# Making all queries early, so that their tiles become slots for VectorE's exponentials, and splitting the end of a kernel of attention and a state-space layer over two engines and two queues

## The chip, the cores and the metric

The kernel runs on one core of one Trainium2 chip. The metric is the device time of one execution in microseconds (us), as the median of several executions. Beside the time there is a trace of one execution of each kernel. Its span, from the first to the last instruction, is shorter than the device time of the same execution (before: 754.8 us).

PE is the tensor engine, PEld its weight loads, DVE is VectorE, ACT is ScalarE, POOL is GpSimd, SP is the engine that issues most DMAs (607 of 611 before).

## The reference, cut to what matters

Two independent layers of 2048 positions and width 640 are computed and laid side by side: a state-space layer (A) and attention (B) with 32 heads of 20 that share one key and one value. (The code is shortened here, not word for word.)

```python
def _B_ref(x, wq, wk, wv, wo):
    q = (x @ wq).reshape(B, S, H, Dh).transpose(0, 2, 1, 3)
    k, v = x @ wk, x @ wv
    p = _softmax(jnp.einsum("bhqd,bkd->bhqk", q, k) * (Dh ** -0.5), axis=-1)
    o = jnp.einsum("bhqk,bkd->bhqd", p, v)
    return o.transpose(0, 2, 1, 3).reshape(B, S, H * Dh) @ wo

return jnp.concatenate([_A_ref(...), _B_ref(...)], axis=-1)     # _A_ref: a linear recurrence over the 2048 positions
```

The scores are 32 x 2048 x 2048 values. In the kernel they are 2048 tiles of 128 keys x 512 queries, and each tile needs an exponential.

## The kernel before: the parts that matter

The kernel is built by a small scheduler of its own. It simulates the five engines with a duration for each operation, writes down the order in which operations start, and emits that order with semaphores. It draws 24 random plans and keeps the one that it reckons shortest. So a change in one place can move instructions everywhere, and the order on each engine is fixed when the kernel is built.

```python
        best = None
        for seed in range(self.PLANS):
            plan = copy.copy(self)
            plan.s = Schedule(seed)
            plan.program()
            try:
                plan.s.run()
            except RuntimeError:
                continue
            end = max(op.end for op in plan.s.order)
            if best is None or end < best[0]:
                best = (end, plan)
        return best[1]
```

Exponentials are made in two ways. ScalarE takes two or three tiles in one instruction, straight from a group of three PSUM banks. VectorE takes single tiles: it writes `max(score + 16256, 0)` as a 16-bit integer, which is read as a bf16 number near the exponential, and three more copies of it, each shifted by a constant. The four versions are each multiplied with their own share of the values, so their errors cancel. Each version needs a holder (`DR`) until the tensor engine has read it.

```python
    CHUNKS = (3, 3)
    MISC = 1
    NPT = 24
    NOP = 7
    NRD = 3
    NDS = 18
    SHARE = 0.25

    SHIFTS = ((0, 0.2421875), (32, 0.201171875), (64, 0.169921875), (96, 0.142578125))
# ...
    def fill_d(self, op, m, bank=None):
        h = self.d_free()[0]
        self.d_count += 1
        b, kc, j = self.score(op, m, bank.ap, bank)
        n = len(self.SHIFTS)
        h.taken, h.left, h.users = True, n, []
        key = f"DR{h.index}"
        first = self.dve(self.ts(p.DR[:, h.index, :], bank.ap, 16256.0, 0.0, ALU.add, ALU.max), 663, deps=[op],
                         reads=[bank.key], writes=[key], prio=self.P1OWN if own else self.P1)
# ...
    def want_d(self, taken=0, own=0):
        s = self.s
        if self.tile_n >= NTILE - 8 or self.d_count + taken + own + 1 > self.SHARE * (self.tile_n - 16):
            return False
        if len(self.d_banks()) <= taken or self.behind():
            return False
        return len(self.d_free()) > taken + own + len(self.SHIFTS) - 1
```

`want_d` says when a tile may go to VectorE: not in the last 8 tiles, only up to a quarter of all tiles (`SHARE`), and only when a holder is free for the first version and each of its copies. There are 18 holders. The copies are made in pairs, by VectorE or by GpSimd.

Queries are made from `xbT` (the transposed input) and `wqf` in four blocks of 512 positions, each one some 300 to 450 tiles ahead of its use, through the buffer `QP`:

```python
        for qb in range(NQB):
            for blk in range(NC):
                t = -98 + blk if qb == 0 else (qb - 1) * 512 + 60 + 40 * blk
```

The last of them comes at tile 1244 of 2048. Until then the three buffers stay in use.

Groups of heads are normalised through DRAM, all but the last one. At the end, the last accumulator is copied out of PSUM into `pvsb`, its sums are turned and inverted on chip, and it is normalised in one piece. Five output tiles are evicted and sent from one queue:

```python
                return e.reciprocal(p.rdT[:], bank.cols(0, 16))
        r = self.dve(rc, 170, deps=[m1], reads=[bank.key], writes=[f"rdT{slot}"], prio=0.45)
        spread = bass.AP(tensor=p.rdT, offset=0, ap=[[16, 128], [1, 16], [0, 32]])
        self.spread_op[b] = self.dve(lambda e: e.tensor_copy(p.rdX[:], spread), 350, deps=[r],
                                      reads=[f"rdT{slot}"], writes=[f"rdX{slot}"], prio=1)
# ...
    def norm_task(self, b, bank):
        p = self
        slot = b % 2
        src = p.pvsb[:, slot, :]
        fns = [self.mm(bank.cols(128 * i, 128 * i + 128),
                       p.rdX[:, 4 * i:4 * i + 4, :].rearrange("p j d -> p (j d)"), p.ident[:], True, True)
               for i in range(4)]
        m2 = self.pe(fns, 4 * 65, deps=[self.spread_op[b], self.c_op["ident"]] + bank.last, prio=1.5,
                     reads=[f"rdX{slot}", "ident"], writes=[bank.key])
        d = self.dve(self.tt(src, src, bank.ap, ALU.mult), 610, deps=[m2],
                     reads=[bank.key, f"pvsb{slot}"], writes=[f"pvsb{slot}"], prio=self.EV)
# ... in finish(), for the last five output tiles:
        if end in (4, 1, 3):
            ev = self.act(lambda e: e.activation(st, bank.ap, ACT.Copy), 600, ...)
        else:
            ev = self.dve(lambda e: e.tensor_copy(st, bank.ap), 620, ...)
# ...
        self.stage_dma[key] = self.dma(fns, 131072, f"out{key}", deps=[ev], reads=[key], prio=1)
```

Of the kernel before, what the change touches and what calls it, by code (L numbers as in the profile page):

```python
# [412 lines left out]
class Build:  # L413
# [5 lines left out]
    NDS = 18  # L419
# [16 lines left out]
    def build(self):  # L436
        nc = self.nc
        with ExitStack() as o:
# [10 lines left out]
            with ExitStack() as p2:  # L449
# [11 lines left out]
                shares.update({f"CT{tb}_{c}": [f"xn{tb}"] for tb in range(2) for c in range(NC)})  # L461
                em = Emitter(nc, plan.s.order, [b.key for b in plan.banks], shares)
# [39 lines left out]
    def alloc(self, o):  # L502
        sb = self.sb
        self.xbT = sb(o, "xbT", [128, NC, S], BF16)
# [5 lines left out]
        self.wqf = sb(o, "wqf", [128, NC * 640], BF16)  # L510
# [6 lines left out]
        self.DR = sb(o, "DR", [128, self.NDS, 512], I16)  # L517
        self.VZ = sb(o, "VZ", [128, 32], BF16)
        self.WO = sb(o, "WO", [128, NC, 640], BF16)
        self.WOt = sb(o, "WOt", [128, 640], BF16)  # L520
# [5 lines left out]
        self.QP = sb(o, "QP", [128, NC, 512], BF16)  # L526
# [10 lines left out]
        self.rdT = sb(o, "rdT", [128, 16], BF16)  # L537
        self.rdX = sb(o, "rdX", [128, 16, 32], BF16)
# [97 lines left out]
    def program(self):  # L636
# [8 lines left out]
        self.evac_op, self.norm_op, self.spread_op = {}, {}, {}  # L645
# [24 lines left out]
        self.s.spawn(self.late_loads())  # L670
        self.free_banks.remove(self.pvbank)
# [4 lines left out]
        self.s.sources["dve"].append(self.copy_source)  # L676
        self.s.sources["pool"].append(self.pool_source)
# [34 lines left out]
    def constants(self):  # L712
# [14 lines left out]
        def select(t, pattern, op, v, base, mult, dur):  # L727
# [24 lines left out]
              for i in range(1, 12)]  # L752
# [11 lines left out]
        self.c_op["WOt"] = self.dve(lambda e: e.memset(p.WOt[:], 0.0), 250, writes=["WOt"], prio=2.5,  # L764
                                    gate=lambda: self.tile_n > 300)

    def loads(self):
# [30 lines left out]
        fns = [lambda e, j=j: e.dma_start(p.WOt[32 * j:32 * j + 20, :], self.wo[560 + 20 * j:580 + 20 * j, :]) for j in range(4)]  # L798
        self.wot_op = self.dma(fns, 102400, "wot", reads=["WOt"], writes=["WOt"], deps=[self.c_op["WOt"]])
# [426 lines left out]
    def want_own(self):  # L1226
        if self.tile_n >= NTILE - 8 or self.d_count + 1 > self.SHARE * (self.tile_n - 16) or self.behind():
            return False
        if sum(1 for o in self.firsts if o.start is None) >= self.WAITING:
            return False  # L1230
        self.firsts = [o for o in self.firsts if o.start is None]
        return len(self.d_free()) > len(self.SHIFTS) - 1
# [82 lines left out]
    def want_d(self, taken=0, own=0):  # L1315
        s = self.s
        if self.tile_n >= NTILE - 8 or self.d_count + taken + own + 1 > self.SHARE * (self.tile_n - 16):
            return False
        if len(self.d_banks()) <= taken or self.behind():
            return False  # L1320
        return len(self.d_free()) > taken + own + len(self.SHIFTS) - 1
# [32 lines left out]
    def fill_d(self, op, m, bank=None):  # L1354
# [12 lines left out]
        first = self.dve(self.ts(p.DR[:, h.index, :], bank.ap, 16256.0, 0.0, ALU.add, ALU.max), 663, deps=[op],  # L1367
# [11 lines left out]
    def pv_entry(self, b, kc, j, k, h, op):  # L1379
        self.pvq[b][j].append((self.VS[:, k, kc, 0:32], kc, self.DR[:, h.index, :].bitcast(BF16), f"DR{h.index}", op, h, "VS"))  # L1380
# [33 lines left out]
    BACKLOG = 9  # L1414

    def pool_source(self):
# [3 lines left out]
        if not can or len(self.d_free()) < 2:  # L1420
            return None
# [7 lines left out]

    def copy(self, op, k, tiles, pool=False):  # L1430
# [5 lines left out]
        def at(x):  # L1436
            if len(x) == 1:
                return p.DR[:, x[0], :]
            return bass.AP(tensor=p.DR, offset=512 * x[0], ap=[[512 * p.NDS, 128], [512 * (x[1] - x[0]), 2], [1, 512]])
        if pool:  # L1440
            def words(x):
                return bass.AP(tensor=p.DR, offset=512 * x[0], ap=[[512 * p.NDS, 128], [512 * (x[1] - x[0]), 2], [1, 512]]).bitcast(I32)
            add = bass.AP(tensor=p.step, offset=k, ap=[[4, 128], [0, 2], [0, 256]])
            op.fns.append(self.tt(words(dst), words(src), add, ALU.add))
            op.reads.append("step")
        else:
# [43 lines left out]
    def pv(self, op, b, group):  # L1490
# [14 lines left out]
        if self.pv_filled[b] == 64 and not any(self.pvq[b]) and not any(self.d_left[b, j] for j in range(4)):  # L1505
            self.pv_b += 1
            slot = b % 2
            ev = self.dve(lambda e: e.tensor_copy(p.pvsb[:, slot, :], bank.ap), 620, deps=[op], reads=[bank.key],
                          writes=[f"pvsb{slot}"], prio=self.PVEV,
                          gate=lambda: b < 2 or self.s.done(self.scat_op[b - 2]))  # L1510
            self.evac_op[b] = ev
            if b < NQB * NGG - 1:
                self.normalize(b, ev)
            self.pv_gate = [ev]
# [17 lines left out]
    def normalize(self, b, ev):  # L1532
# [6 lines left out]
        sd = o = self.dma(lambda e: e.dma_start(sums, p.pvsb[20:117:32, slot, :]), 4096, f"sum{slot}", land=self.LATE_DMA, deps=[ev], reads=[pv],  # L1539
# [11 lines left out]
        for blk, parts in self.rows_of(b).items():  # L1551
            at, rd = (NC * qb + blk) % self.NOP, (NC * qb + blk) % self.NRD
            zero = []
            if b == NQB * NGG - 2 and blk == NC - 1:
# [4 lines left out]
            self.scat_op[b].append(self.dma(fns, 1024 * sum(x[3] for x in parts), f"OP{at}", issue=770.0, deps=[ev] + zero, reads=[pv], writes=[f"OP{at}"],  # L1559
# [8 lines left out]
            if rows == 128 or zero:  # L1568
                self.norm_op[NC * qb + blk] = self.dve(
                    self.tt(p.OP[0:rows, at, :], p.OP[0:rows, at, :], p.rdP[0:rows, rd, :], ALU.mult), 350,  # L1570
                    deps=self.rd_op[NC * qb + blk], port=True, reads=[f"OP{at}", f"rdP{rd}"], writes=[f"OP{at}"], prio=self.EV)
# [7 lines left out]
    def den_task(self, b, bank):  # L1579

        p = self
        slot = b % 2
        src = p.pvsb[:, slot, :]
        m1 = self.pe([self.mm(bank.cols(4 * i, 4 * i + 4), src[:, 128 * i:128 * i + 128], p.E1[:], True, True)
                      for i in range(4)], 4 * 65, deps=[self.evac_op[b], self.c_op["E1"]] + bank.last, prio=1.5,
                     reads=[f"pvsb{slot}", "E1"], writes=[bank.key])

        def rc(e):
            with p.nc.allow_low_precision("bf16 reciprocal of softmax denominator"):
                return e.reciprocal(p.rdT[:], bank.cols(0, 16))  # L1590
        r = self.dve(rc, 170, deps=[m1], reads=[bank.key], writes=[f"rdT{slot}"], prio=0.45)
        spread = bass.AP(tensor=p.rdT, offset=0, ap=[[16, 128], [1, 16], [0, 32]])
        self.spread_op[b] = self.dve(lambda e: e.tensor_copy(p.rdX[:], spread), 350, deps=[r],
                                      reads=[f"rdT{slot}"], writes=[f"rdX{slot}"], prio=1)
        yield lambda: r.start is not None
        bank.last = [r]
        self.give(bank)

    def norm_task(self, b, bank):
        p = self  # L1600
        slot = b % 2
        src = p.pvsb[:, slot, :]
        fns = [self.mm(bank.cols(128 * i, 128 * i + 128),
                       p.rdX[:, 4 * i:4 * i + 4, :].rearrange("p j d -> p (j d)"), p.ident[:], True, True)
               for i in range(4)]
        m2 = self.pe(fns, 4 * 65, deps=[self.spread_op[b], self.c_op["ident"]] + bank.last, prio=1.5,
                     reads=[f"rdX{slot}", "ident"], writes=[bank.key])
        d = self.dve(self.tt(src, src, bank.ap, ALU.mult), 610, deps=[m2],
                     reads=[bank.key, f"pvsb{slot}"], writes=[f"pvsb{slot}"], prio=self.EV)
        self.norm_op[NC * NQB] = d  # L1610
# [4 lines left out]
    def o_task(self, qb, k, bank):  # L1615
# [6 lines left out]
        for blk in range(NC):  # L1622
            at = (NC * qb + blk) % self.NOP
            steps.append((NC * qb + blk, p.OP[:, at, :], p.WO[:, blk, :], [f"OP{at}", "WO"]))
        if last:
            slot = (NQB * NGG - 1) % 2
            steps.append((NC * NQB, p.pvsb[:, slot, :], p.WOt[:], [f"pvsb{slot}", "WOt"]))

        def part(i, prev):
# [3 lines left out]
            for ts in range(4) if k == 4 else [k]:  # L1633
                out, ww = (bank.cols(128 * ts, 128 * ts + 128), w[:, 512:640]) if k == 4 else (bank.ap, w[:, 0:512])
                fns.append(self.mm(out, src[:, 128 * ts:128 * ts + 128], ww, i == 0 and ts in (0, k), end))
            return self.pe(fns, 4 * 65 if k == 4 else self.mmt(512), deps=[self.norm_op[n], self.wo_op, self.wot_op] + bank.last,
                           prev=prev, prio=1.4 if last and end else 2.5 if last else self.task_prio(),
                           reads=keys, writes=[bank.key])
        for i in range(len(steps)):
            if last:  # L1640
                yield lambda: steps[i][0] in self.norm_op
            prev = part(i, prev)
# [6 lines left out]
        self.give(bank)  # L1649

    def finish(self, prev, rows, bank, ops, end=None):
# [10 lines left out]
        if end in (4, 1, 3):  # L1662
            ev = self.act(lambda e: e.activation(st, bank.ap, ACT.Copy), 600, deps=[prev], reads=[bank.key], writes=[key], prio=1)
        else:
# [8 lines left out]
        self.stage_dma[key] = self.dma(fns, 131072, f"out{key}", deps=[ev], reads=[key], prio=1)  # L1673
# [375 lines left out]
    SSM_FROM, SSM_TO, Y_STEP, GRACE = 260, 1850, 20, 40  # L2049
    unit_due = {}  # L2050

    def background(self):
        T = self.tasks
        T.append((-100, 1, lambda: all((0, c) in self.xb_op for c in range(NC)), lambda bank: self.qt_task(bank)))
        for qb in range(NQB):
            for blk in range(NC):
                t = -98 + blk if qb == 0 else (qb - 1) * 512 + 60 + 40 * blk
                T.append((t, 1, lambda qb=qb, blk=blk: self.q_ready(qb, blk), lambda bank, qb=qb, blk=blk: self.q_task(qb, blk, bank)))
            T.append((t + 0.5, 0, lambda qb=qb: self.row_ready(qb), lambda bank, qb=qb: self.row_task(qb, bank)))
        for b in range(NQB * NGG):  # L2060
            if b == NQB * NGG - 1:
                T.append((64 * (b + 1), 0, lambda b=b: self.den_ready(b), lambda bank, b=b: self.den_task(b, bank)))
                T.append((64 * (b + 1), 0, lambda b=b: b in self.spread_op and self.s.done([self.spread_op[b]]),
                          lambda bank, b=b: self.norm_task(b, bank)))
        for qb in range(NQB):
            for k in range(5):
                T.append((512 * (qb + 1) + 30 + 40 * k if qb < NQB - 1 else NTILE - 8, 2, lambda qb=qb: self.o_ready(qb),
                          lambda bank, qb=qb, k=k: self.o_task(qb, (4, 0, 1, 2, 3)[k], bank)))
        jobs = []
# [25 lines left out]
    def den_ready(self, b):  # L2095
        return b in self.evac_op and self.s.done([self.evac_op[b]])

    def o_ready(self, qb):
        blks = range(NC if qb < NQB - 1 else 1)
# [97 lines left out]
```

## Time and profile before

| | before |
|---|---|
| time, median of 4 | 758.48 us (758.28 to 758.72) |
| span of the traced execution | 754.8 us |
| first exp starts | 21.57 us |
| exps on ScalarE | 419 of two tiles, 247 of three: 1579 tiles |
| tiles on VectorE | 469 |
| last exp ends | 742.29 us |

Two lines of the page of the kernel before. The first has the busy time of each engine, its share of the span and its instructions. The second has the chain of work that ended last, by engine.

```profile
PE 711.4 (94%) x11441; PEld 260.3 (34%) x11442; DVE 649.7 (86%) x1301; ACT 732.2 (97%) x692; POOL 432.4 (57%) x455
...
ACT 80%; PE 16%; DVE 3%; issue 1%; POOL 0%; DVEq 0%
```

ScalarE is busy nearly all the time, and following the waits back from the last instruction one is on ScalarE for 80% of the span. So ScalarE's stream of exps sets the time, and what other engines do costs time only where it makes an exp start late.

The groups of instructions of the kernel before, by shape. The columns are line, engine, operation, tiles, shapes and count, then busy time and mean ns of one, then the idle time before them and what ended it.

```profile
L628 POOL TENSOR_TENSOR DR<-DR,step 128x512 int32<-128x512 int32 x407 | 413.2, 1042 | 292.8 <-DVE DR L633 197.5 <-PE MB L618 29.1 <-DVE g L1950 19.2
L1177 ACT ACTIVATE PR<-SC 128x1024 bf16<-128x1024 f32 x419 | 407.9, 1149 | 3.2 <-PE SC L618 2.8 <-PE MB L618 0.2
L1177 ACT ACTIVATE PR<-SC 128x1536 bf16<-128x1536 f32 x247 | 351.7, 1603 | 0.4 <-PE MB L618 0.4
L633 DVE TENSOR_SCALAR DR<-SC 128x512 int16<-128x512 f32 x404 | 272.5, 687 | 53.3 <-PE SC L618 40.1 <-PE MB L618 8.3 <-POOL DR L628 1.1
...
L633 DVE TENSOR_SCALAR DR<-DR 128x1024 int16<-128x1024 int16 x269 | 106.8, 442 | 11.4 <-PE MB L618 10.4
...
L633 DVE TENSOR_SCALAR DR<-MB 128x512 int16<-128x512 f32 x65 | 44.1, 679 | 2.4 <-PE MB L618 2.3
```

The mean of an exp (1149 ns) is not what it costs, because consecutive exps overlap: the shortest of two tiles lasts 1.017 us, longer than the 0.904 from its start to the next one's. The start times in the trace say more: back to back, an exp of two tiles is followed by the next after 0.904 us and one of three after 1.331 us. The 666 exps thus need 419 x 0.904 + 247 x 1.331 = 707.5 us. From the first exp's start to the last one's it took more than that: summed over all pairs of neighbours, the starts came 12.8 us later than back to back. I call these 12.8 us the late starts. The remaining 12.6 us are what comes after the last exp.

That end is in the timeline of the kernel before. The columns are start, duration, engine, line and operation with tiles, then in brackets the idle time before and its releaser. An `x12` stands for twelve instructions in a row.

```profile
740.20 4.00 DVE L633 TENSOR_SCALAR DR<-DR 128x1024 int16<-128x1024 int16 x12 [0.22 <-PE MB L618]
...
744.77 0.69 DVE L1508 CAST pvsb<-MB 128x512 bf16<-128x512 f32 x1 [0.58 <-PE MB L618]
...
746.28 0.43 DVE L1593 COPY rdX<-rdT 128x512 bf16<-128x512 bf16 x1
...
747.26 0.69 DVE L628 TENSOR_TENSOR pvsb<-pvsb,SC 128x512 bf16<-128x512 bf16 x1 [0.23 <-PE SC L614]
...
748.46 0.60 ACT L1663 ACTIVATE PR<-MB 128x512 bf16<-128x512 f32 x1 [6.17 <-PE MB L614]
...
748.68 1.34 DVE L1665 CAST PR<-SC 128x512 bf16<-128x512 f32 x2 [0.73 <-PE SC L614]
...
749.09 2.43 SPq L1672 DMA_DIRECT2D out_dram<-PR  x5
...
749.76 0.60 ACT L1663 ACTIVATE PR<-SC 128x512 bf16<-128x512 f32 x1 [0.21 <-PE SC L614]
```

The last exp ended at 742.29. VectorE still made copies until 744.2, so the accumulator could only be copied out at 744.77. The reciprocal, a spread copy and a multiplication follow in a chain, then five evictions until 750.36, while one queue issues the five outputs one after the other until 751.5.

### The profile page before, as it was taken

Reading aid. Unit: us, or ns where it says so; the run is one execution under the profiler, and the core shown is the slowest. Engines: PE = TensorE matmul, PEld = TensorE weight load, DVE = VectorE, ACT = ScalarE, POOL = GpSimd, SP = SyncE. Lnnn points to the kernel's source line nnn. Section 1 sums busy time; section 2 is a strip of 40 time slices with the busy share of each in tenths; the row PEclk is TensorE's granted clock in tenths of the full one; section 3 lists DMA queues with packets and bytes.
Section 4 is the critical chain, followed back from the end, with each engine's and each line's share of the span. In section 5 each row is a group of like instructions: output and inputs, shape, how many; then the busy total and the mean of one; then the engine's idle time right before and its main releaser. Section 6 shows DMA issues by size and latency. Waiting matters only on the chain.

```text
span 754.8 us, 26719 instructions
## 1 busy us (share of the span) xinstructions
PE 711.4 (94%) x11441; PEld 260.3 (34%) x11442; DVE 649.7 (86%) x1301; ACT 732.2 (97%) x692; POOL 432.4 (57%) x455
## 2 busy tenths in 40 slices
PE   9998988888999999999899999998999999999996
PEld 4332222244433532333343333332443233343323
DVE  7879999999988698788989889889898999887885
ACT  5899999999999999999999999999999999999994
POOL 3775565503755255587555675545665656756781
PEclk9999999999999999999999999999999999999999
DMA  9436544311220011101100101112000010000001
GB/s 199 87 89 151 118 120 87 72 21 25 46 47 15 23 32 56 41 18 29 41 16 12 39 30 38 36 31 50 15 19 14 12 39 17 23 19 26 14 25 42
DMA packets 78484, 34.59 MB, mean 46 GB/s; under 512 B 59080, under 2 KB 78368, under 8 KB 78368
## 3 DMA queue, kind: packets, MB, share of 16 engines
q1 hardware_dynamic: 77036, 32.76, 17.9%
q8 instruction: 91, 1.49, 0.8%
q10 hardware_dynamic: 1332, 0.13, 0.2%
q14 instruction: 25, 0.20, 0.1%
HBM read 11.59 MB, written 9.76 MB: 28 GB/s over the span
## 4 chain that ended last, share of the span: by engine, by line
ACT 80%; PE 16%; DVE 3%; issue 1%; POOL 0%; DVEq 0%
ACT PR L1177 79%; PE MB L618 5%; PE SC L618 5%; PE MB L614 4%; PE SC L614 1%; DVE DR L633 1%; DVE prod L628 1%; DVE CT L628 0%; DVE W L633 0%; PE SC L902 0%; DVE g L1950 0%; DVE CT L632 0%; POOL DR L628 0%; DVE CA L628 0%; DVE CA L632 0%
## 5 line engine op out<-in xcount | busy, mean ns | idle before, releaser
L1177 ACT ACTIVATE PR<-SC 128x1024 bf16<-128x1024 f32 (+1 forms) x666 | 718.0, 1317 | 3.6 <-PE SC L618 2.8
L628 POOL TENSOR_TENSOR DR<-DR,step 128x512 int32<-128x512 int32 x407 | 413.2, 1042 | 292.8 <-DVE DR L633 197.5
L633 DVE TENSOR_SCALAR DR<-SC 128x512 int16<-128x512 f32 x404 | 272.5, 687 | 53.3 <-PE SC L618 40.1
L618 PE MATMUL SC<-QT,KT 32*128 32x512 bf16 x1983 | 260.6, 384 | 31.9 <-ACT PR L1177 25.9
L618 PE MATMUL MB<-DR,VS 128*32 128x512 bf16 x1876 | 223.0, 384 | 0.9 <-POOL DR L628 0.5
L618 PE MATMUL MB<-PR,VP 128*32 128x512 bf16 x1579 | 208.8, 384 | 2.6 <-ACT PR L1177 1.1
L618 PEld LDWEIGHTS SC<-QT,KT 32*128 32x128 bf16 x1983 | 66.9, 91 | 257.7 <-ACT PR L1177 185.7
L633 DVE TENSOR_SCALAR DR<-DR 128x1024 int16<-128x1024 int16 (+1 forms) x324 | 120.7, 421 | 13.3 <-PE MB L618 12.1
L618 PEld LDWEIGHTS MB<-DR,VS 128*32 128x32 bf16 x1876 | 55.8, 94 | 67.1 <-issue 38.2
L618 PEld LDWEIGHTS MB<-PR,VP 128*32 128x32 bf16 x1579 | 53.7, 94 | 56.8 <-issue 36.2
L614 PE MATMUL MB<-CT,W 128*32 128x320 bf16 (+2 forms) x1040 | 52.2, 301 | 0.7 <-DVE prod L628 0.4
L633 DVE TENSOR_SCALAR DR<-MB 128x512 int16<-128x512 f32 x65 | 44.1, 679 | 2.4 <-PE MB L618 2.3
L614 PE MATMUL MB<-xaT,BT 128*32 128x256 bf16 x800 | 33.3, 274 | 0.0
L618 PE MATMUL MB<-KT,VZ 128*32 128x256 bf16 x628 | 33.0, 274 | 0.0
L614 PE MATMUL MB<-xaT,BA 128*32 128x256 bf16 x800 | 32.3, 274 | 0.3 <-DVE DR L633 0.3
L628 DVE TENSOR_TENSOR prod<-MB,tab 128x1024 bf16<-128x1024 f32 x20 | 24.4, 1220 | 8.7 <-PE MB L614 8.7
L614 PE MATMUL MB<-CA,W 128*32 128x512 bf16 (+1 forms) x640 | 30.7, 302 | 0.6 <-DVE prod L628 0.5
L614 PEld LDWEIGHTS MB<-CT,W 128*32 128x32 bf16 x1040 | 21.2, 96 | 18.9 <-issue 10.0
L1665 DVE CAST stg<-MB 128x512 bf16<-128x512 f32 x35 | 23.9, 682 | 3.0 <-PE MB L614 2.6
L1950 DVE TENSOR_TENSOR_SCAN g<-sc,hst,prod 128x256 bf16<-128x256 f32 x30 | 26.3, 883 | 0.0
L618 PE MATMUL MB<-QT,KT 32*128 32x512 bf16 x65 | 24.9, 384 | 0.0
L614 PE MATMUL MB<-WO,OP 128*32 128x128 bf16 (+1 forms) x560 | 24.5, 290 | 0.0
(150 smaller groups left out, 443.1 us busy)
## 6 DMA issues: line engine op xcount, KB each, us to landing
out_dram<-stg SPq DMA_DIRECT2D x31, 128.0 KB, 1.8
qd<-QP SPq DMA_DIRECT2D x20, 128.0 KB, 1.9
QT<-qd SPq DMA_DIRECT2D x28, 80.0 KB
OP<-pvsb SPq DMA_DIRECT2D x108, 20.0 KB
rdP<-recs SPq DMA_DIRECT2D x108, 20.0 KB
W<-in_A_B_re_dram SPq DMA_DIRECT2D x10, 160.0 KB, 2.7
W<-in_A_B_im_dram SPq DMA_DIRECT2D x10, 160.0 KB, 3.2
lbd<-W SPq DMA_DIRECT2D x10, 160.0 KB, 2.0
```

The lines of the kernel that those rows point to most:

```text
L614: r = e.matmul(out[32 * j:32 * j + 32], lhsT=lhsT[:, 32 * j:32 * j + 32], rhs=rhs, start=start, stop=stop, tile_position=(0, 32 * j), skip ...
L618: return lambda e: e.matmul(out, lhsT=lhsT, rhs=rhs, start=start, stop=stop, **kw)
L628: return lambda e: e.tensor_tensor(out, a, b, op)
L633: return lambda e: e.tensor_scalar(out, a, s1, s2, op0=op0, op1=op1)
L1177: ex = self.act(lambda e: e.activation(dst, t[:, 0:512 * n], ACT.Exp, scale=1.0 / UNIT), 0.8333 * 512 * n + 64, table="exp", deps=[op], re ...
L1665: ev = self.dve(lambda e: e.tensor_copy(st, bank.ap), 620, deps=[prev], reads=[bank.key], writes=[key], prio=self.EV, gate=(lambda: last.e ...
L1950: o = self.dve(lambda e, ri=ri, init=init: e.tensor_tensor_scan(p.g[:, u, ri, :], rdec, p.prod[:, 1, 0, ri, :], init, ALU.mult, ALU.add), ...
```

## The change

Its intent: all four blocks of queries are due by tile 250. Then `wqf`, `QP` and most of `xbT` are dead, and 21 more holders are laid over them (`MORE`), beside two more of the old kind. With 41 holders instead of 18, VectorE can take more tiles. At the end, the last two head groups are normalised on chip, three of the five last outputs are computed early but for the last group and kept as partial sums, the last copy out of PSUM and the last normalisation are halved, VectorE takes no tile in the last 20, and two of the five outputs go out from ScalarE's queue.

```diff
-    NDS = 18
+    NDS = 20
+    MORE = 21
@@ alloc: one buffer for xbT, wqf, QP and the holders; the added holders lie over the first three
+        self.BIG = sb(o, "BIG", [128, ends[3]], BF16)
+        self.xbT = self.BIG[:, 0:ends[0]].rearrange("p (c n) -> p c n", c=NC)
+        self.wqf = self.BIG[:, ends[0]:ends[1]]
+        self.QP = self.BIG[:, ends[1]:ends[2]].rearrange("p (c n) -> p c n", c=NC)
+        self.dr_at = [ends[2] + 512 * i for i in range(self.NDS)]
+        # ... 10 in xbT, 6 in wqf, 5 in QP
@@ new: the holders join once the last queries are made
+    def more(self):
+        yield lambda: NQB - 1 in self.row_mm and self.s.done([self.row_mm[NQB - 1]]) \
+            and all(self.s.done([self.qd_op[NQB - 1, i]]) for i in range(NC))
+        self.dhold += [Holder(self.NDS + i) for i in range(self.MORE)]
@@ want_own, want_d
-        if self.tile_n >= NTILE - 8 or ...
+        if self.tile_n >= NTILE - self.LAST or ...          # LAST = 20
@@ background
-                t = -98 + blk if qb == 0 else (qb - 1) * 512 + 60 + 40 * blk
+                t = -98 + blk if qb == 0 else self.Q_FROM[qb] + self.Q_STEP * blk   # (0, 30, 110, 190), 15
-    SSM_FROM, SSM_TO, Y_STEP, GRACE = 260, 1850, 20, 40
+    SSM_FROM, SSM_TO, Y_STEP, GRACE = 260, 1780, 20, 40
@@ pv: the last accumulator leaves PSUM in two halves
+                self.evac_op[b] = [
+                    self.act(lambda e: e.activation(p.pvsb[:, slot, 0:256], bank.cols(0, 256), ACT.Copy), 390, ...),
+                    self.dve(lambda e: e.tensor_copy(p.pvsb[:, slot, 256:512], bank.cols(256, 512)), 350, ...)]
-            if b < NQB * NGG - 1:
+            if b < NQB * NGG - 2:
                 self.normalize(b, ev)
@@ den_task: no spread copy; the matrix unit reads the reciprocals with a step of 0; two halves
-        self.spread_op[b] = self.dve(lambda e: e.tensor_copy(p.rdX[:], spread), 350, ...)
+                    col = bass.AP(tensor=p.rdT, offset=16 * slot + 4 * i + j, ap=[[32, 128], [0, 32]])
@@ finish
-        if end in (4, 1, 3):
+        if end in (1, 3):
             ev = self.act(lambda e: e.activation(st, bank.ap, ACT.Copy), 600, ...)
+        elif end is not None:
+            ev = self.dve(self.tt(st, bank.ap, self.partial(end), ALU.add), 630, ...)
-        ... self.dma(fns, 131072, f"out{key}", deps=[ev], reads=[key], prio=1)
+        ... self.dma(fns, 131072, f"out{key}", deps=[ev], reads=[key], prio=1, eng=ev.eng if end == 1 or end == 3 else "sp")
```

Cut: the shifting of two head groups into the small weight tile `WOt`, the bookkeeping of two keys for a halved tile, `o_task` with its early part, a stop of GpSimd's copies in the last 10 tiles (`POOL_LAST`), a copy on ScalarE after the last tile.

## The prediction

> **What bounds it now.** The span is 754.8 us. On the page ACT is 97% busy (PE 94%, DVE 86%, POOL 57%), and the chain that ended last is 79% the exp line. From the trace: first exp at 21.57 us, last exp ends at 742.29. Of 2048 score tiles ScalarE takes 1579, as 419 exps of two tiles and 247 of three. Back to back they start 0.904 and 1.331 us apart: 707.6 us; the other 12.8 us are late starts (3.6 us of them idle in the waits). [...] Only moving tiles off ScalarE, or shortening the 12.5 us after the last exp, helps. The other 469 tiles are VectorE's: one 0.687 us op from PSUM and three shifted copies, made in pairs by DVE (0.42 us) or POOL (1.04 us).
>
> **What the change does** (instruction order of both builds): early queries free the input, wq and query buffers, so holders go from 18 to 41. VectorE tiles rise from 469 to 498 (cap 512). ScalarE has 470 exps of two, 203 of three, one of one: 424.9 + 270.2 + 0.5 = 695.6 us, 12.0 less, all on the chain. DVE gains 29 x 0.687 = 20 us of first ops, 40 pair copies (17 us), three partial-output evictions: about +40, to 690 of 743 us, 93%. POOL goes from 407 to 418 pairs. More pairs are not adjacent, which costs nothing: both forms took 0.42 us.
>
> **The end** (timeline): from last exp to the cast of pvsb 2.5 us, as 12 copies still run; cast 0.69, sums, reciprocal, 0.43 spread copy, 0.69 multiply; output matmuls and five evictions to 750.36; five output DMAs issued in a row on one queue, the last 0.74 us after the last eviction; then 3.3 us to landing and end. After: VectorE tiles stop 20 before the end instead of 8 (-1.0), the cast is halved over two engines (-0.3), no spread copy (-0.5), three evictions become adds to early partial sums but stay a chain of three on DVE (0), three queues (-0.5). About 2.3 us less.
>
> **Against it.** DVE at 93% has half its former slack. PE scores of a slot wait for the DVE op that empties its third bank (34 us of such waits, hidden behind the other slot). Queries are packed early, near where PE was 99% busy (200 to 300 us, table of windows). I allow 3 us of new late exps. [...]
>
> **Sum.** 21.57 + 695.6 + 12.8 + 3 + 10.2 = 743.2 us of span; the timed median lies 3.8 us above the profiled span, so 747.0 us. Range 743.0 to 752.0. Chances: over 2% faster 0.16, within 2% 0.83, slower 0.01.
>
> **What would show each step.** Exp counts 470/203; last exp ending near 733 us; late starts 13 to 19 us; DVE near 690 us busy; 10 to 11 us after the last exp; output issues on ACT's queue too.
>
> **What would make it wrong.** DVE late in bursts, with runs of two-tile exps each needing 0.69 us plus copies within 0.904 us: then PE waits, exps start late, and the 12 us shrink. If fewer matmuls compete late, the lags may fall and the gain pass 2%. The three DVE adds may stretch the end.

The sum is: 743.2 us of span, 747.0 us of time. The 3 us of late exps in it is an allowance of mine, and the 0.5 us for the exp of one tile an estimate (0.904 less the 0.427 from two tiles to three); no trace showed them.

## The result, and the profile after

The change takes 748.25 us in the median of four (747.54 to 750.88) against 758.48 for the kernel before. The ratio is 0.9871, with a 95% interval of 0.9847 to 0.9896. Here and below a ratio is the mean time of one kernel's runs over that of the other's of the same rounds, so it is not quite the ratio of the medians quoted. It is 1.3% faster, within the 2% that count as the same, and within the predicted range.

The page of the kernel after, the same two lines:

```profile
PE 710.7 (95%) x11325; PEld 256.3 (34%) x11325; DVE 665.3 (89%) x1360; ACT 721.6 (97%) x700; POOL 446.0 (60%) x466
...
ACT 70%; PE 26%; DVE 3%; issue 0%; DVEq 0%
```

ScalarE still sets the time, though the chain now passes the tensor engine more often (26% instead of 16%). VectorE is 15.6 us busier than before, not 40.

The groups of instructions of the kernel after. `BIG` is now the buffer of the holders.

```profile
L1197 ACT ACTIVATE PR<-SC 128x1024 bf16<-128x1024 f32 x470 | 445.0, 1107 | 6.6 <-PE SC L635 6.1 <-PE MB L635 0.2
L645 POOL TENSOR_TENSOR BIG<-BIG,step 128x512 int32<-128x512 int32 x418 | 426.7, 1050 | 270.1 <-DVE BIG L650 116.6 <-DVE g L2025 73.3 <-PE MB L635 19.2
L650 DVE TENSOR_SCALAR BIG<-SC 128x512 int16<-128x512 f32 x456 | 303.7, 686 | 41.7 <-PE SC L635 34.9 <-PE MB L635 3.2
L1197 ACT ACTIVATE PR<-SC 128x1536 bf16<-128x1536 f32 x203 | 281.9, 1602 | 0.4 <-PE SC L635 0.4
...
L650 DVE TENSOR_SCALAR BIG<-BIG 128x1024 int16<-128x1024 int16 x309 | 115.6, 429 | 8.6 <-PE MB L635 4.7 <-POOL BIG L645 2.9
...
L650 DVE TENSOR_SCALAR BIG<-MB 128x512 int16<-128x512 f32 x42 | 28.5, 678 | 1.1 <-PE MB L635 1.1
```

VectorE has 456 + 42 = 498 tiles, 29 more; GpSimd makes 418 pairs of copies instead of 407, and VectorE 309 instead of 269. ScalarE has 51 more exps of two tiles and 44 fewer of three, and one of a single tile (0.477 us, an estimate: 0.904 less the 0.427 from two tiles to three): 470 x 0.904 + 203 x 1.331 + 0.5 = 695.5 us, 12.0 less. The idle time before exps went up, from 3.6 to 7.0 us, and nearly all of it waits for the tensor engine's scores (`PE SC`).

The end in the timeline of the kernel after, in which the last exp ended at 736.46:

```profile
737.61 0.38 ACT L1564 ACTIVATE pvsb<-MB 128x256 bf16<-128x256 f32 x1 [1.15 <-PE MB L635]
738.02 0.42 DVE L1566 CAST pvsb<-MB 128x256 bf16<-128x256 f32 x1 [1.88 <-ACT pvsb L1564]
...
739.62 0.75 DVE L645 TENSOR_TENSOR pvsb<-pvsb,SC 128x256 bf16<-128x256 bf16 x2 [0.51 <-PE SC L635]
...
740.54 1.89 DVE L645 TENSOR_TENSOR PR<-SC,BA 128x512 bf16<-128x512 f32 x3 [0.18 <-PE SC L631]
...
740.76 0.60 ACT L1735 ACTIVATE PR<-SC 128x512 bf16<-128x512 f32 x1 [2.77 <-PE SC L631]
...
741.26 1.59 SPq L1747 DMA_DIRECT2D out_dram<-PR  x3
741.39 0.37 ACTq L1747 DMA_DIRECT2D out_dram<-PR  x1
...
742.06 0.60 ACT L1735 ACTIVATE PR<-SC 128x512 bf16<-128x512 f32 x1 [0.70 <-PE SC L631]
742.69 0.37 ACTq L1747 DMA_DIRECT2D out_dram<-PR  x1
```

Nothing is left to copy after the last exp, and the two halves leave PSUM 1.15 us after it. The halves don't run at once, though. VectorE's half starts only when ScalarE's is done: its wait of 1.88 us is put down to `ACT pvsb`. The two queues issue side by side, and the last issue comes 0.03 us after the last eviction.

Set side by side, in us after the last exp's end:

| | before | after | difference |
|---|---|---|---|
| first copy of the last accumulator starts | 2.48 | 1.15 | -1.33 |
| last eviction ends | 8.06 | 6.20 | the step from the row above: -0.53 |
| last output issued (start) | 8.78 | 6.23 | -0.69 |
| end of the span | 12.56 | 9.73 | -0.28 |

The whole span now adds up. Before: 21.6 until the first exp + 707.5 of exps + 12.8 late + 12.6 = 754.5. After: 22.9 + 695.5 + 17.7 + 9.7 = 745.8. (The missing 0.3 to 0.4 us is that an exp ends a little later than its successor could start: the last one before lasts 1.287 us against a step of 0.904, the last one after 0.785 against the 0.477 estimated.) The change won 12.0 us in the exps and 2.8 at the end; it lost 4.9 in late starts, and the first exp came 1.3 us later. What the last two are was the open question.

### The profile page after: what moved, and what is told of

It reads as the page before. It is cut to its first block, busy times and chain, and to the rows that moved or that the text cites. A ratio compares the mean times of both kernels' runs of the same rounds, so it can differ in the third digit from the quotient of the medians.

```text
span 746.2 us, 26653 instructions
## 1 busy us (share of the span) xinstructions
PE 710.7 (95%) x11325; PEld 256.3 (34%) x11325; DVE 665.3 (89%) x1360; ACT 721.6 (97%) x700; POOL 446.0 (60%) x466
## 4 chain that ended last, share of the span: by engine, by line
ACT 70%; PE 26%; DVE 3%; issue 0%; DVEq 0%
ACT PR L1197 70%; PE MB L635 8%; PE SC L635 8%; PE MB L631 8%; PE SC L631 1%; DVE prod L645 1%; DVE W L650 0%; DVE CT L645 0%; DVE CA L645 0%; PE SC L922 0%; DVE CT L649 0%; DVE CA L649 0%; DVE g L2025 0%; DVE BIG L650 0%; DVE stg L1740 0%
## 5 line engine op out<-in xcount | busy, mean ns | idle before, releaser
L1197 ACT ACTIVATE PR<-SC 128x1024 bf16<-128x1024 f32 (+1 forms) x674 | 707.4, 1255 | 7.1 <-PE SC L635 6.5
L645 POOL TENSOR_TENSOR BIG<-BIG,step 128x512 int32<-128x512 int32 x418 | 426.7, 1050 | 270.1 <-DVE BIG L650 116.6
L650 DVE TENSOR_SCALAR BIG<-SC 128x512 int16<-128x512 f32 x456 | 303.7, 686 | 41.7 <-PE SC L635 34.9
L635 PE MATMUL SC<-QT,KT 32*128 32x512 bf16 x2006 | 264.5, 385 | 26.5 <-ACT PR L1197 19.4
L635 PE MATMUL MB<-BIG,VS 128*32 128x512 bf16 x1992 | 249.4, 383 | 0.3
L635 PE MATMUL MB<-PR,VP 128*32 128x512 bf16 x1550 | 219.9, 385 | 1.1 <-DVE pvsb L1559 0.5
L650 DVE TENSOR_SCALAR BIG<-BIG 128x1024 int16<-128x1024 int16 (+1 forms) x349 | 124.7, 415 | 8.6 <-PE MB L635 4.7
L635 PEld LDWEIGHTS MB<-BIG,VS 128*32 128x32 bf16 x1992 | 62.4, 95 | 65.4 <-issue 42.4
L650 DVE TENSOR_SCALAR BIG<-MB 128x512 int16<-128x512 f32 x42 | 28.5, 678 | 1.1 <-PE MB L635 1.1
L631 PE MATMUL MB<-BIG 128*32 128x512 bf16 x320 | 23.4, 382 | 0.0
L631 PEld LDWEIGHTS MB<-xaT,BA 128*32 128x32 bf16 x800 | 18.5, 96 | 11.8 <-issue 6.8
```

The source lines that it names most:

```text
L631: r = e.matmul(out[32 * j:32 * j + 32], lhsT=lhsT[:, 32 * j:32 * j + 32], rhs=rhs, start=start, stop=stop, tile_position=(0, 32 * j), skip ...
L635: return lambda e: e.matmul(out, lhsT=lhsT, rhs=rhs, start=start, stop=stop, **kw)
L645: return lambda e: e.tensor_tensor(out, a, b, op)
L650: return lambda e: e.tensor_scalar(out, a, s1, s2, op0=op0, op1=op1)
L1197: ex = self.act(lambda e: e.activation(dst, t[:, 0:512 * n], ACT.Exp, scale=1.0 / UNIT), 0.8333 * 512 * n + 64, table="exp", deps=[op], re ...
```

## The experiments

Twelve kernels ran, three rounds each. All gave a correct result. The table has what each trace shows, in us; the rows of `before` and `after` are the first traces, from above. "Half clock" is the time, before the last exp, in which the trace's clock records grant the tensor engine half its clock.

| kernel | VectorE tiles | first exp | exps | late starts | after the last exp | span | half clock |
|---|---|---|---|---|---|---|---|
| before | 469 | 21.57 | 707.5 | 12.8 | 12.6 | 754.8 | 3.4 |
| e9 before again | 469 | 22.90 | 707.5 | 14.3 | 12.5 | 757.7 | 6.8 |
| e10 before, plan 2 | 465 | 22.78 | 709.3 | 17.9 | 11.7 | 762.1 | 6.8 |
| after | 498 | 22.85 | 695.5 | 17.7 | 9.7 | 746.2 | 6.8 |
| e4 after again | 498 | 22.48 | 695.5 | 17.2 | 9.7 | 745.3 | 6.8 |
| e1 end only | 468 | 22.13 | 708.1 | 19.4 | 10.4 | 760.3 | 10.2 |
| e2 no added holders | 476 | 22.78 | 704.8 | 17.3 | 10.1 | 755.2 | 6.8 |
| e3 late queries | 481 | 22.77 | 702.8 | 16.0 | 10.1 | 751.9 | 6.8 |
| e5 one output queue | 498 | 22.14 | 695.5 | 16.2 | 10.6 | 744.8 | 3.4 |
| e6 VectorE tiles to the end | 500 | 22.63 | 694.7 | 21.6 | 10.7 | 749.8 | 13.7 |
| e7 after, plan 2 | 495 | 22.32 | 696.9 | 21.0 | 9.3 | 749.9 | 10.2 |
| e8 after, plan 4 | 498 | 22.43 | 695.5 | 16.9 | 9.7 | 744.9 | 3.4 |
| e11 queries earlier | 497 | 22.24 | 696.0 | 20.3 | 9.3 | 748.2 | 10.2 |
| e12 true first-op time | 500 | 22.57 | 694.7 | 21.3 | 9.1 | 747.9 | 13.7 |

### e1: the new end alone

```diff
-    NDS = 20
-    MORE = 21
+    NDS = 18
+    MORE = 0
-    Q_FROM, Q_STEP = (0, 30, 110, 190), 15
+    Q_FROM, Q_STEP = (0, 60, 572, 1084), 40
-    SSM_FROM, SSM_TO, Y_STEP, GRACE = 260, 1780, 20, 40
+    SSM_FROM, SSM_TO, Y_STEP, GRACE = 260, 1850, 20, 40
```

> The changed kernel with 18 holders and none added later, the old query times and the old end of the state-space work: only the new end stays. Its build has 468 VectorE tiles (422 exps of two, 245 of three, about 708 us of exps, as before). Theory A (the holders give the gain in the middle, the end gives about 2.8 us): late starts of exps near 12.8 us as before, 9.7 us after the last exp, so about 755.5 us, ratio about 0.996. Rival B (most of the gain is in the end): ratio about 0.988, as the whole change.

Measured: 760.7 us, ratio 1.0042 (1.0017 to 1.0068). My expectation of 755.5 was wrong, and so was the rival's. The end came out nearly as expected (10.4 us, 2.2 less than before), and the exps too (708.1). But the late starts are 19.4 us instead of 12.8. This kernel has as few VectorE tiles as the one before and its late queries. This trace has 10.2 us of half clock against 3.4, but clock is not all of it: the executions of this kernel at a mean clock of 0.995 took 760.3 to 761.0 us, those of the kernel before at that clock 758.4 to 759.5. So neither more VectorE tiles nor early queries are needed for late starts of this size.

### e2: no added holders

```diff
-    MORE = 21
+    MORE = 0
```

> The changed kernel without the 21 added holders (20 stay); queries are still early. Its build has 476 VectorE tiles (441 exps of two, 230 of three, about 705 us of exps, 9.7 us more than the change). Theory A: about 7 to 10 us slower than the change, near 756 us. Rival C (early queries alone free PE later, the holders add little): within 3 us of the change. Late starts of exps: if early queries cause the 4.9 us of added late starts they are near 17 us here too; if the higher VectorE load does, near 13 to 14 us.

Measured: 754.62 us, ratio 0.9964 (0.9936 to 0.9991), so 7.4 us slower than the change measured in the same rounds (e4, 747.20). That is theory A's expectation of 7 to 10, at a time 1.4 us below the 756 named. The groups of exps and of first operations of this kernel, to be held against those of the change:

```profile
L1197 ACT ACTIVATE PR<-SC 128x1024 bf16<-128x1024 f32 x441 | 422.5, 1109 | 6.2 <-PE SC L635 5.6 <-PE MB L635 0.4
...
L1197 ACT ACTIVATE PR<-SC 128x1536 bf16<-128x1536 f32 x230 | 322.1, 1585 | 0.3 <-PE SC L635 0.3
L650 DVE TENSOR_SCALAR BIG<-SC 128x512 int16<-128x512 f32 x426 | 285.4, 685 | 55.9 <-PE SC L635 46.7 <-PE MB L635 5.4
...
L650 DVE TENSOR_SCALAR BIG<-MB 128x512 int16<-128x512 f32 x50 | 33.8, 677 | 0.5 <-PE MB L635 0.4
```

VectorE has 426 + 50 = 476 tiles and ScalarE 441 x 0.904 + 230 x 1.331 = 704.8 us. The late starts (17.3) and the end (10.1) are nearly those of the change. Counting first operations per 50 us, the added holders pay soonest after they appear: 41 against 33 between 250 and 300 us, 36 against 29 in the next 50. So the holders move 22 tiles, which is 9.2 us of exps. In total late starts don't grow with them. In one stretch they do: between 250 and 300 us they are 1.7 us in the change and 0.9 here.

### e3: queries late, so holders late

```diff
-    Q_FROM, Q_STEP = (0, 30, 110, 190), 15
+    Q_FROM, Q_STEP = (0, 60, 572, 1084), 40
```

> The changed kernel with the queries at their old, late times, so that the 21 holders come only after about 1250 of the 2048 tiles. Its build has 481 VectorE tiles (450 exps of two, 222 of three, about 702.5 us of exps, 7 us more than the change). Theory A: about 752 to 754 us, between the kernel without added holders and the change. Rival C (early queries themselves matter through late starts): the difference to the change is not 5 to 7 us but more, with late starts above 18 us.

Measured: 753.75 us, ratio 0.9943 (0.9913 to 0.9973): 6.5 us slower than the change (e4), as the 7.2 us of additional exps ask for, and at the lower edge of the late starts seen in the changed kernel (16.0). Early queries matter because the holders come early. They may also have a price: the stop of 1.63 us near 191 us, of which more below, is absent here. No exp between 150 and 200 us is later than 0.61 us.

### e4: the change again

> The change itself on the same chip: about 748 us, ratio 0.987. If the first exp at 22.85 instead of 21.57 us in the first profile was only a later arrival of the input, it may be at 21.6 us here; if the change causes it, it is near 22.8 us again.

Measured: 747.20 us, ratio 0.9857 (0.9829 to 0.9884). The first exp came at 22.48 us, between the two values I had named, so this run alone did not decide. The late starts sit at the same places in the plan as in the first trace (1.63 us at 191.0 there, 1.64 at 190.4 here, and so on), which says that they are part of the plan and not chance.

### e5: one output queue

```diff
-        ... prio=1, eng=ev.eng if end == 1 or end == 3 else "sp")
+        ... prio=1, eng="sp")
```

> The change with all five last outputs issued from one queue again; the plan is otherwise the same (470/203/1 exps). If the two queues are worth what the traces suggest (last issue 0.03 us after the last eviction instead of 0.72), the tail after the last exp grows from 9.7 to about 10.2 to 10.4 us; all else the same, so about 0.5 to 0.7 us slower than the change. Rival: the end is bound by the landing of the last output alone, and nothing changes.

Measured: 747.83 us, ratio 0.9877 (0.9839 to 0.9915). The time doesn't resolve it, the trace does. The last output is issued 0.59 us after the last eviction instead of 0.03, and the end takes 10.6 us instead of 9.7. Two queues are worth 0.8 us here, of which my estimate had 0.5.

### e6: VectorE tiles to the end

```diff
-    LAST = 20
+    LAST = 8
```

> The change with VectorE tiles allowed until 8 tiles before the end, as before, instead of 20. Its build has 500 VectorE tiles and 694.3 us of exps, 0.8 us less. Theory: copies are left over after the last exp, and the cast of the last accumulator starts about 2.0 to 2.5 us after the last exp instead of 1.15, so the tail is about 10.7 us; in all within 1 us of the change. Rival (the earlier cast comes from the early partial sums and not from stopping early): the cast starts at 1.1 us again.

Measured: 751.47 us, ratio 0.9914 (0.9882 to 0.9946). The end is as expected: copies are left over (two of them on ScalarE), the accumulator leaves PSUM 2.12 us after the last exp, and the end takes 10.7 us. The timeline of this kernel, in which the last exp ended at 739.10:

```profile
738.96 1.17 ACT L1494 ACTIVATE BIG<-BIG 128x512 int16<-128x512 int16 x2
...
741.22 0.38 ACT L1564 ACTIVATE pvsb<-MB 128x256 bf16<-128x256 f32 x1 [1.10 <-PE MB L635]
```

So stopping early is worth 1.0 us at the end. But the kernel is about 3.5 us slower than the change by the medians (of other rounds), not within 1 us: its late starts are 21.6 us, with 13.7 us of half clock, of which more below.

### e7 and e8: other plans of the changed kernel

```diff
-        for seed in range(self.PLANS):
+        for seed in range(2, 3):          # e8: range(4, 5)
```

> The change with one other plan of its 24 random ones (the second), not the one that its builder judged best. Its build has 495 VectorE tiles and 696.9 us of exps, 1.4 us more. If late starts (17.7 us in the change, 12.8 before) belong to the single plan, they differ here by several us and the stops of the change, 1.6 us at 191 us among them, are elsewhere; then the added 4.9 us are partly luck of the draw. If VectorE's load causes them, they are again 17 to 19 us, and the time is about 750 us.

> The change with another of its 24 plans (the fourth): 498 VectorE tiles, 695.5 us of exps, as the change. Same two theories as for the second plan: late starts of 17 to 19 us and about 749 us if load causes them; several us apart from that if they belong to the plan.

Measured: plan 2 takes 753.10 us (ratio 0.9938, 0.9907 to 0.9969), plan 4 takes 748.00 (0.9887, 0.9843 to 0.9931). Late starts are 21.0 and 16.9 us. Between two plans of one kernel there are 4.1 us of late starts and 5 us of time, though plan 2's trace also has 6.8 us more of half clock. But I had expected the stop of 1.6 us near 191 us to be elsewhere. It is in both (2.1 us at 187.1, 1.9 at 187.9). Plan 4 says little here: on ScalarE and VectorE it follows the change's order of instructions until after 370 us. Plan 2 leaves that order at 61 us and still has the stop, so it doesn't belong to one plan alone.

### e9 and e10: the kernel before again, and another plan of it

No edit for e9; e10 draws only plan 2, as e7 does.

> The kernel before, traced once more: 707.5 us of exps and 12.5 us after the last exp, as in its first trace. If the first exp at 21.6 us and late starts of 12.8 us belong to the kernel, they are the same here; if that trace was a lucky one (its execution took 756.7 us, the timed ones 758.5), the first exp is near 22.4 us or the late starts near 14.5 us, with longer stretches of half clock.

> The kernel before with the second of its 24 plans instead of the one its builder judged best: 465 VectorE tiles, 709.3 us of exps, 1.8 us more. If late starts belong to the single plan, they are several us above 12.8, as in the changed kernel's plan 2 (21.0), and the time is about 763 us; if they belong to the change, they stay near 13 us and the time is about 760 us.

Measured: e9 takes 758.24 us (ratio 0.9984, 0.9956 to 1.0012). Its traced execution took 759.50. The first exp is at 22.90 us, and late starts are 14.3 us. So the first trace of the kernel before was a lucky one, and a first exp at 22.8 us has nothing to do with the change. e10 takes 763.64 us (1.0049, 1.0012 to 1.0085), and its late starts are 17.9 us with the smallest VectorE load of all (639 us busy, 84%). Large late starts thus come with the old kernel too, when another of its plans is taken. Part of that is clock: its one execution at a mean clock of 1.000 took 758.47 us, 2.4 to 2.7 more than those of the kernel before at that clock, of which the exps are 1.8.

### e11: queries earlier still

```diff
-    Q_FROM, Q_STEP = (0, 30, 110, 190), 15
+    Q_FROM, Q_STEP = (0, 20, 70, 120), 10
```

> The change with its queries earlier still (the last block from tile 120 on instead of 190, steps of 10): 497 VectorE tiles, 695.5 us of exps, as the change. If queries that run into the start of the state-space work make the stop of 1.6 us at 191 us (absent with late queries), it is smaller here and the time 1 to 2 us less than the change; if the stop is only the burst of VectorE work there, it stays and the time is that of the change, 747 to 748 us.

Measured: 749.62 us, ratio 0.9877 (0.985 to 0.9904). The stop is still there (1.98 us at 187.8, with a half-clock stretch from 186.9 on). So moving the queries away from the start of the state-space work doesn't remove it. The second reading, a burst of VectorE work, stands, but it doesn't say why the kernels with late queries lack the stop.

### e12: the builder told the true time of the first operation

```diff
-        first = self.dve(self.ts(self.dr(h.index), ...), 663, deps=[op],
+        first = self.dve(self.ts(self.dr(h.index), ...), 610, deps=[op],
-    SHARE = 0.25
+    SHARE = 0.28
```

> The change with its builder told that VectorE's first op takes 0.61 us (the trace shows 0.598 us from one to the next back to back; the builder reckons 0.663) and a cap of 28 per cent instead of 25: 500 VectorE tiles, 694.7 us of exps, 0.8 us less. If VectorE's time is what holds the tiles back, this gains 1 to 2 us on the change; if late starts decide, it is within plan to plan noise, 746 to 752 us.

Measured: 749.64 us, ratio 0.9868 (0.9837 to 0.9898), indistinguishable from the change. It has 500 VectorE tiles, two more. VectorE's reckoned time is not what keeps the number there. What does is open; caps of 26 to 30 per cent with the old reckoned time also built plans with no more than 493 tiles (built, not run).

None of these versions beats the change by more than the noise.

### What the late starts are

Two things can be seen in the traces.

First, the stop near 191 us. The timeline of the kernel after:

```profile
187.17 0.39 PE L635 MATMUL MB<-QT,KT 32*128 32x512 bf16 x1
...
187.74 0.49 DVE L645 TENSOR_TENSOR CT<-W,CT 128x640 bf16<-128x640 bf16 x1
...
187.86 0.39 PE L635 MATMUL SC<-QT,KT 32*128 32x512 bf16 x3 [0.30 <-ACT PR L1197]
...
188.60 0.42 DVE L645 TENSOR_TENSOR prod<-prod 128x512 bf16<-128x512 bf16 x1
...
189.08 0.68 DVE L650 TENSOR_SCALAR BIG<-MB 128x512 int16<-128x512 f32 x1
...
189.82 0.73 PE L631 MATMUL MB<-xaT,BA 128*32 128x256 bf16 x20 [1.57 <-DVE BIG L650]
...
190.59 0.39 PE L635 MATMUL SC<-QT,KT 32*128 32x512 bf16 x3
...
191.03 1.02 ACT L1197 ACTIVATE PR<-SC 128x1024 bf16<-128x1024 f32 x1 [0.96 <-PE SC L635]
```

After its scores at 187.86 the tensor engine waits 1.57 us for `BIG`, the first operation of a VectorE tile: that tile's scores, written at 187.17, hold the PSUM bank that the next matmuls (`MB<-xaT,BA`) need. The operation stands on VectorE behind a row of state-space work (`CT`, `W`, `prod`) and starts only at 189.08. In the tensor engine's built order the next scores for ScalarE stand behind these matmuls, so they come only at 190.59, and the exp at 191.03 starts 1.63 us late. My prediction named this kind of stop (VectorE late in a burst). But it comes where there are the fewest VectorE tiles: 14 first operations between 150 and 200 us, against 27 to 48 in the stretches after it, and by the operand addresses of the built program no added holder is used before 207 us. The load of the added tiles is not its cause.

Early queries may be. Late starts between 150 and 200 us come to 1.05 to 1.41 us in all five traces with late queries (before, e1, e3, e9, e10) and to 1.95 to 2.24 in the five with early ones in which no half clock falls there (after, e2, e4, e6, e12). But e2, e4 and e6 keep the change's order on ScalarE until 205 us or later, and e12, whose order differs from 42 us on, has no single stop over 1.02 us. So few plans are compared, and the cause is not shown.

Second, the clock. The clock records have stretches of 3.4 us, or multiples (3.413 us before, 6.827 after), in which the tensor engine gets half its clock (0.50). The changes of clock lie on a grid: in the first traces of before and after all of them, and in e6 the seven from 24.161 to 747.787 us, lie whole multiples of 3.413 us apart. Here is the beginning in the kernel before (first fence, with the window ahead of it), in the one after (second) and in e9 (third), in tables by window: the columns are the window, its length, then for PE, PEld, DVE, ACT and POOL busy time and count, the granted clock, the share of the DMA engines and GB/s.

```profile
21.70:25.10 3.40, 2.87 (x35) 1.64 (x38) 2.60 (x19) 3.40 (x4) 3.11 (x7) 1.00 0.34 70
25.10:28.60 3.50, 3.50 (x28) 0.65 (x24) 2.60 (x8) 2.80 (x4) 3.19 (x7) 0.51 0.49 116
```

```profile
24.70:31.50 6.80, 6.66 (x48) 1.29 (x48) 3.27 (x16) 5.00 (x6) 6.05 (x14) 0.50 0.36 86
```

```profile
24.80:31.60 6.80, 6.71 (x48) 1.27 (x48) 3.17 (x16) 4.94 (x6) 6.05 (x14) 0.50 0.38 91
```

Before had one such stretch just after its first exps, after and e9 had two. Up to 52 us, late starts came to 2.2 us before, 3.9 after and 3.7 in e9. This part of the 4.9 us, about 1.5, is not the change's.

More stretches come later in some runs. In e5 the stretch falls on the stop near 190 us (in e7, e8 and e11 too), in e6 there is one at 396 us, and in e12 one at 505 us. The windows ahead of them are shown too:

```profile
183.50:186.90 3.40, 1.53 (x32) 0.74 (x28) 3.33 (x10) 2.94 (x3) 0.00 (x0) 1.00 0.00 0
186.90:190.30 3.40, 3.40 (x45) 1.06 (x37) 2.08 (x4) 1.98 (x2) 2.88 (x3) 0.50 0.00 0
```

```profile
392.80:396.20 3.40, 2.39 (x32) 0.68 (x33) 3.37 (x6) 3.23 (x3) 2.34 (x2) 1.00 0.13 28
396.20:399.60 3.40, 3.40 (x33) 1.00 (x35) 1.61 (x5) 2.82 (x3) 1.04 (x1) 0.50 0.12 28
```

```profile
501.90:505.30 3.40, 2.38 (x22) 0.60 (x19) 3.40 (x8) 3.37 (x5) 1.65 (x3) 0.99 0.17 43
505.30:512.10 6.80, 6.46 (x64) 1.81 (x61) 6.09 (x13) 5.93 (x6) 4.70 (x5) 0.50 0.13 30
```

In each of these three cases the 3.4 us ahead have little work on the tensor engine: 1.5 to 2.4 us busy, 22 to 32 matmuls. But little work is neither needed for such a stretch nor enough. Ahead of the first stretch of the kernel before the tensor engine was busy for 2.87 of 3.40 us. And e1 has a window, 47 steps of 3.413 us after its clock change at 25.40 us, that is as thin and keeps its full clock after it:

```profile
185.80:189.20 3.40, 2.07 (x26) 0.73 (x26) 3.33 (x7) 3.40 (x4) 1.24 (x2) 1.00 0.02 5
189.20:192.60 3.40, 3.40 (x81) 1.83 (x77) 3.37 (x9) 3.40 (x5) 0.00 (x0) 1.00 0.01 4
```

Nor does the plan fix the place: e5 has the change's order of instructions up to its last outputs, yet its half clock falls at 186.9 us and not at 24.7.

e6 then has two exps late by 0.72 and 0.73 us at 399.0 and 400.7, where the change, without that stretch, has none over 0.02 between 394 and 405 us. In the traces of the changed kernel and its variants, late starts go with the time at half clock: 16.2 and 16.9 us with 3.4 us of it, 16.0 to 17.7 with 6.8, 19.4 to 21.0 with 10.2, 21.3 and 21.6 with 13.7. They don't go with VectorE's load: e10 with 639 us of VectorE work has 17.9, e2 with 646 has 17.3, the change with 665 has 17.7. The half clock also goes with the spread of the times. Of 25 executions of the kernel before, the three with a mean clock of 1.000 took 755.8 to 756.1 us, the nine with 0.994 took 758.9 to 759.7, and one with 0.990 took 761.8. From end to end that is 0.8%, more than half of what the change gained. What starts a half-clock stretch was not tried by an edit and stays open; the windows above don't settle it.

Held against e9, which has the same half clock as the first trace of the change, the account is: exps -12.0, late starts +3.4, the end -2.8, the first exp 0.0, together -11.4 of the 11.5 us between their spans. Of the 3.4 us, 0.86 lie between 150 and 200 us, where the stop is, and 1.1 between 250 and 300. These two parts are not one plan's luck: e7 and e12, which leave the change's order before 62 us, have them too (0.6 to 2.3 us more than e9 in the first stretch, 1.3 to 1.7 in the second). In the second, all eight traces in which the added holders come early have 1.73 to 2.27 us, and the six others 0.61 to 1.55. So about 2 us seem to come with early queries and early holders, though no run isolates that. The other 1.4 us may be the plan's: the kernel before, with another plan (e10), has 3.6 us more than e9 without any of the change. Why the best of 24 plans happened to be a good one before and a middling one after stays open.

## Why the prediction was right

- **Exps, -12.0 us.** Predicted 695.6, measured 695.5. It followed from the counts of the built program and two intervals of the old trace, which the chip repeated (0.904 and 1.331 us again).
- **The end, -2.3 us.** Measured -2.8. The mechanism was right but for one part: the halved copy out of PSUM, from which 0.3 us was expected, took 0.83 us from the first start to the last end instead of 0.69. The sizes were -1.33 instead of -1.0 for the copies left over, -0.53 instead of -0.8 for the chain to the last eviction, in which the two halves didn't run at once, -0.69 instead of -0.5 for the queues, and -0.28 after the last issue, which was not foreseen. e5 and e6 confirm the queues (0.8) and the early stop (1.0) one by one.
- **Late starts, +3 us.** Measured +4.9, or +3.4 with like clock. The size was nearly right but the step "DVE at 93% has half its former slack" failed. VectorE was 665 us busy (89%), not 690, and in total late starts don't follow its load. They go with the half clock and differ between plans, and about 2 us of them lie where the early queries and holders are.
- **VectorE's +40 us** was mis-sized; it measured +15.6. The first operations gave 272.5 + 44.1 to 303.7 + 28.5, +15.6 instead of 20, mostly because an operation that lasts 0.686 us is followed by the next after 0.598 (29 x 0.598 = 17.3): the mean duration counts the overlap twice. The copies gave +3.7 instead of +17. The pairs went from 106.8 to 115.6 us, and single copies fell from 55 to 40, which I missed since 15 shifts of queries have the same names in the built program. The other groups together gave -3.7.
- **The offset of 3.8 us between span and time** was the wrong term of the sum. Within one execution it is 1.7 to 1.9 us. The rest was that the traced execution of the kernel before was 1.7 us faster than its timed ones; the trace of e9, whose execution took 759.50, has twice its half clock. So I added some 1.7 us too much, and that hid most of what the span had too little: 743.2 predicted, 746.2 measured, of which 1.3 was the first exp, 1.9 the late starts and 0.3 the end of the last exp, left out of the sum, less 0.5 at the end.
- **Non-adjacent pairs, and copies beside GpSimd's.** The pairs over two places cost nothing, as predicted: their median is 0.421 us (259 pairs) against 0.420 for adjacent ones (10) before, 0.418 (294) against 0.415 (15) after. Some pair copies took far longer. Of those that VectorE started while GpSimd was at one, all 29 before and 18 of 21 after ended 0.28 to 0.41 us after GpSimd's. The longest, 1.27 us at 563.96 before, started 0.24 us into one. (The other three lie within GpSimd copies recorded as 2.6 us long.) No run was made for the cause, and it is not shown. The effect is small here: over 0.418 us each, VectorE's pair copies took 6.5 us more before and 3.3 after.

So the time came out right, 748.25 against 747.0, partly by luck: two errors had opposite signs.

## What to carry to other kernels

When one engine's stream sets the time, write the span as first start, back-to-back work, late starts and tail; counts of the built program times intervals from start to start gave the second to a tenth of a microsecond here (695.6 predicted, 695.5 measured). Take the cost of pipelined instructions from those intervals, not from durations, which overlap (here 0.904 us from start to start against a mean duration of 1.149). Before explaining a few microseconds of late starts by the change, trace the old kernel twice and one other draw of its plan: here chance and plan alone gave as much as the change seemed to have lost. Then compare stretch by stretch: what every plan of the new kernel has and no plan of the old one speaks for the change.
